# One retention kernel, two changes to its state: full-array products become two quarter-array products, and four small state updates become two

## The chip, the cores and the metric

The kernel runs on one core of a Trainium2 chip. The metric is the device time of one execution in microseconds; a profiled execution also gives the span from its first to its last instruction. The engines are named as in the profile: PE is the matrix engine (PEld its weight loads), DVE the vector engine, ACT the scalar engine, POOL the fourth compute engine, SP the engine that issues all transfers here.

## The reference, cut to what matters

```python
# q, k, v: (4, 8, 768, 64); w_in 512x2048, w_out 2048x512, twice
state = zeros((B, H, D, D))
for t in range(S):
    state = gamma[h] * state + k_t (outer) v_t
    y[:, :, t] = scale * (q_t @ state)
x = y as (B*S, H*D)                     # 3072 tokens x 512
x = leaky_relu(x @ w_in) @ w_out        # first block, factor 0.01
x = elu(x @ w_in2) @ w_out2             # second block
```

Here gamma is 1 - 2^(-5-h) for head h. The weights arrive as 64-bit floats and are converted on the chip.

## The kernel before, in words

**The dense part.** The 3072 tokens are handled in 6 blocks of 512. Each step takes one of 16 slices of 128 hidden features: `gemm1` makes h from the block's x (12 products), `leaky` or the elu functions make g, `split_g` splits it into a high and a low part, and `gemm2`, one to three steps later in `drain`, multiplies by the second weight (12 products). A pair of `gemm1` and `gemm2` is 24 products of 512 columns.

**The retention part.** It runs in chunks of 128 tokens: 24 chunks, 6 of them to a sequence, and for each chunk two units of four heads, so 48 units w = 0 to 47. Unit w has chunk c = w // 2, and i = w % 2 says which two pairs of heads. A unit is written in two halves. `att_a` multiplies queries and keys into scores `sc` (four products, rows 0 to 63 of the array for one head of a pair, rows 64 to 127 for the other) and DVE multiplies them with the mask into `pt`. `att_b` adds up the output `o` in PSUM: q times the state of the chunk before (line 384, only where the chunk is not a sequence's first), then `pt` times v (line 387), and beside it the new k-v product of the chunk (line 391, not for a sequence's last chunk). ACT copies the output to `xhi`, DVE updates the state `st` (line 399, or line 402 where it begins) and then writes `xlo` (line 403). `prep_q` and `prep_k` scale q and k on POOL.

`st` holds for each of the four pairs of heads a 128x128 matrix whose two diagonal 64x64 quarters are the states of the two heads; the other two quarters are zeros, written once on POOL at the start. One product with it serves both heads, and the update has four instructions in a unit, one for each head:

```python
for p, a, r, rs in pairs:               # rs: partitions and columns of head r
    nc.vector.scalar_tensor_tensor(out=st[rs, a, rs], in0=st[rs, a, rs], scalar=gamma[2 * a + r] ** C,
                                   in1=o[rs, p, 1, :D], op0=ALU.mult, op1=ALU.add)
```

**The order.** Every engine works through its instructions in the order of the program. `att_step` runs `att_a` of unit w+1 and `att_b` of unit w, with operations of `conv` between them: `conv` converts the first block's weights, chunk by chunk (16 chunks; lines 95 to 120, on ACT, DVE and POOL). Units 0 to 7 come before any dense step, units 8 to 15 lie two to a step in the first four dense steps, and the other 32 come one to a step or one to two steps from visit 3 on (a visit is a run of steps on one block of tokens). `load_w` and `att_load` issue the transfers of weights (`raw`) and of k, q, v (`kv`) on SP, in program order; the load of `kv` for chunk 6 waits there for chunk 4 to be done, and the fifth `raw` is behind it. `warm` issues products whose result nobody reads, two at the start and one after each of units 0 and 1; they read `st`.

Of the kernel before, what the change touches and what calls it, by code (L numbers as in the profile page):

```python
# [19 lines left out]
F32 = mybir.dt.float32  # L20
# [6 lines left out]
ALU = mybir.AluOpType  # L27
PSUM = bass.MemoryType.PSUM

B, H, S, D = 4, 8, 768, 64  # L30
DM, DFF = 512, 2048
P = 128
C = 128
# [3 lines left out]
NP = H // 2  # L37
BLK = 512
# [4 lines left out]
HM = MF // 2  # L43
# [8 lines left out]
@with_exitstack  # L52
def body(ctx: ExitStack, tc: tile.TileContext, kkv, w1, w2, tabs, out):
    nc = tc.nc
    gamma = [1.0 - 2.0 ** (-5.0 - h) for h in range(H)]

    big = ctx.enter_context(tc.tile_pool(name="big", bufs=1))
    wp = ctx.enter_context(tc.tile_pool(name="wp", bufs=1))
    cv = ctx.enter_context(tc.tile_pool(name="cv", bufs=2))
# [250 lines left out]
    with ExitStack() as actx:  # L310
        ab = actx.enter_context(tc.tile_pool(name="ab", bufs=1))
        ap_ = actx.enter_context(tc.tile_pool(name="ap", bufs=2))
        aps = actx.enter_context(tc.tile_pool(name="aps", bufs=1, space=PSUM))
        kv, pt = {}, {}
        st = ab.tile([P, NP, P], F32, name="st")
        nc.gpsimd.memset(st, 0.0)
        tab = ab.tile([P, H * C + NP * C + H], F32, name="tab")
        ktab = tab[:, :H]
        mask = tab[:, H : H + H * C].rearrange("p (i r t) -> p i r t", i=2, r=2)
        qtab = tab[:, H + H * C :].rearrange("p (a t) -> p a t", a=NP)  # L320

        def att_load(c, first=0, last=4):

# [7 lines left out]
        def prep_k(w):  # L331
            c, i = divmod(w, 2)
            if c < NCH and c % NCB < NCB - 1:
                k = kv[c][:, 2, 4 * i * D : 4 * (i + 1) * D].rearrange("p (h d) -> p h d", h=4)
                nc.gpsimd.tensor_tensor(k, k, ktab[:, 4 * i : 4 * i + 4].unsqueeze(2).to_broadcast([P, 4, D]), ALU.mult)
# [35 lines left out]
        def att_b(w):  # L371

            c, i = divmod(w, 2)
            cb = c % NCB
            t = pt.pop(w)
            if w < 2 * CPB and i:
                o = ps.tile([P, 2, 2, C], F32, tag="y2", name="o")
            else:
                o = aps.tile([P, 2, 2, C], F32, tag="o", name="o")
            pairs = [(p, 2 * i + p, r, slice(r * D, (r + 1) * D)) for p in range(2) for r in range(2)]  # L380
            if cb:
                q = qd.pop(w)
                for p in range(2):
                    nc.tensor.matmul(o[:, p, 0, :], st[:, 2 * i + p, :], q[:, p, :], start=(p == 0), stop=False, skip_group_check=True)  # L384
            for p, a, r, rs in pairs:
                v = kv[c][:, 3, a * C + r * D : a * C + (r + 1) * D]
                nc.tensor.matmul(o[rs, p, 0, :], v, t[:, r, p * C : (p + 1) * C], start=(cb == 0 and p == 0), stop=True, skip_group_check=True)  # L387
            if cb < NCB - 1:
                for p, a, r, rs in pairs:
                    hs = slice(a * C + r * D, a * C + (r + 1) * D)  # L390
                    nc.tensor.matmul(o[rs, p, 1, :D], kv[c][:, 2, hs], kv[c][:, 3, hs], start=False, stop=True, skip_group_check=True)
            b, ts = c // CPB % 2, slice(c % CPB * C, (c % CPB + 1) * C)
            ks = slice(2 * i, 2 * i + 2)
            nc.scalar.copy(xhi[b][:, ks, ts], o[:, :, 0, :])
            yield
            if cb < NCB - 1:
                for p, a, r, rs in pairs:
                    if cb:
                        nc.vector.scalar_tensor_tensor(out=st[rs, a, rs], in0=st[rs, a, rs], scalar=gamma[2 * a + r] ** C,  # L399
                                                       in1=o[rs, p, 1, :D], op0=ALU.mult, op1=ALU.add)  # L400
                    else:
                        nc.vector.tensor_copy(st[rs, a, rs], o[rs, p, 1, :D])
            nc.vector.tensor_tensor(xlo[b][:, ks, ts], o[:, :, 0, :], xhi[b][:, ks, ts].bitcast(F32), ALU.subtract)  # L403
            yield

# [13 lines left out]
        def att_step(before=0, between=0):  # L419


            nonlocal au
            w = au
            c, i = divmod(w, 2)
            scores = att_a(w + 1) if w + 1 < NU else iter((0, 0))
            outputs = att_b(w)
            next(scores)
            conv(before)
            next(scores)
            prep_q(w + 2)  # L430
            next(outputs)
            conv(between)
            next(outputs)
            prep_k(w + 1)
            c_split()
            if i and CPB <= c < NCH - 2:
                att_load(c + 2)
            au += 1

        def warm(n):  # L440

            t = ps.tile([P, BLK], F32, tag="h", name="idle")
            for _ in range(n):
                nc.tensor.matmul(t, st[:, 0, :], st.rearrange("p a e -> p (a e)"), start=True, stop=True)

        au = 0
        warm(2)
        prep_k(0)
        for _ in att_a(0):
            pass  # L450
        for w, (n1, n2) in enumerate(((0, 1), (0, 1), (1, 0), (1, 1), (0, 1), (1, 1), (0, 1), (1, 1))):
            att_step(n1, n2)
            if w < 2:
                warm(1)
# [5 lines left out]
        for s in range(NA):  # L460
            ph, j, m, (_, _, m0, m1, vi) = steps[s]
            n = units.get(vi, 0)
            h = ps.tile([P, BLK], F32, tag="h", name="h")
# [27 lines left out]
    with ExitStack() as ectx:  # L491
# [44 lines left out]
        for s in range(NA, 2 * NS):  # L536
            ph, j, m, (_, _, m0, m1, vi) = steps[s]
            if s % 4 == 0:
                h = ps.tile([P, BLK], F32, tag="h", name="h")
            else:  # L540
                h = eps.tile([P, BLK], F32, tag="h2", name="h2")
# [13 lines left out]
            if (ph, vi) in comes:  # L555
                nx, i = comes[ph, vi], m // 2
# [9 lines left out]
def _tables():  # L566

    gamma = 1.0 - 2.0 ** (-5.0 - np.arange(H, dtype=np.float64))
    t = np.arange(C)
    scale = 1.0 / np.sqrt(D)  # L570
    d = t[None, :] - t[:, None]
    mask = np.where(d >= 0, scale * gamma[:, None, None] ** np.maximum(d, 0), 0.0)
    qtab = scale * gamma[:, None] ** (t + 1.0)
    ktab = gamma[:, None] ** (C - 1.0 - t)
    tab = np.zeros((P, H * C + NP * C + H), np.float32)
    tab[:, :H] = ktab.T

    mask = mask.reshape(2, 2, 2, C, C).transpose(3, 0, 2, 1, 4)
    tab[:, H : H + H * C] = mask.reshape(P, H * C)
    rows = np.repeat(qtab.reshape(NP, 2, 1, C), D, axis=2).reshape(NP, P, C)  # L580
    tab[:, H + H * C :] = rows.transpose(1, 0, 2).reshape(P, NP * C)
    return tab


# [33 lines left out]
```

## Time and profile before

| | |
|---|---|
| time, median of 3 runs | 1206.05 us (1205.2 to 1210.15) |
| the profiled execution's own time | 1206.01 us |
| its span | 1204.2 us |
| mean granted PE clock | 0.989 |
| PE busy | 1172.1 us, 97% of the span |
| DVE, ACT, POOL busy | 682.6, 544.6, 167.8 us |

The busy times are sums over stretches with different limits, so they are to be read stretch by stretch. Products are pipelined, and one product of 32-bit operands (not of the rounded kind that the dense part uses) stands as two records in the trace: the 80 products of line 384 are 160 records.

### The profile page before, as it was taken

What the parts mean: (1) busy time and instruction counts of PE and PEld (TensorE: products, weight loads), DVE (VectorE), ACT (ScalarE), POOL (GpSimd) and SP (SyncE); (2) the same over time, 40 slices, a digit from 0 to 9 for tenths busy, and PEclk for the clock granted to TensorE, in tenths of its full rate; (3) what the DMA queues carried; (4) which work ended last, traced back from release to release, by engine and by line L of the source; (5) the groups of instructions that cost most, each with busy time, mean ns of one, the idle gap of its engine ahead of it and who ended that gap; (6) DMA issues with size and microseconds to landing.
All of it is one profiled execution on the core that took longest, in us unless ns stands there. A gap on an engine that the chain in (4) does not pass through costs nothing.

```text
span 1204.2 us, 14902 instructions
## 1 busy us (share of the span) xinstructions
PE 1172.1 (97%) x5864; PEld 949.1 (79%) x5864; DVE 682.6 (57%) x1169; ACT 544.6 (45%) x913; POOL 167.8 (14%) x145
## 2 busy tenths in 40 slices
PE   6798899999999999999999999999999999999998
PEld 4576778877777777877888888888888888888887
DVE  5988871424564556364211365666665665666665
ACT  2445542222443444343222455555555555564554
POOL 2566520101332133132000000000000000000000
PEclk8799999999999999999999999999999999999999
DMA  9156030333553355352255610000000010000000
GB/s 374 71 222 268 1 99 7 106 105 123 193 192 140 140 193 184 131 188 94 62 182 193 225 54 18 35 18 18 35 18 18 36 35 1 35 1 1 36 1 35
DMA packets 32822, 117.10 MB, mean 97 GB/s; under 512 B 3184, under 2 KB 3184, under 8 KB 25712
## 3 DMA queue, kind: packets, MB, share of 16 engines
q1 hardware_dynamic: 32752, 116.15, 26.7%
q8 instruction: 46, 0.75, 0.3%
q14 instruction: 24, 0.20, 0.0%
HBM read 84.68 MB, written 31.46 MB: 96 GB/s over the span
## 4 chain that ended last, share of the span: by engine, by line
PE 81%; DVE 11%; ACT 4%; DMA 2%; issue 2%; SPq 0%; ACTq 0%; DVEq 0%
PE h L227 37%; PE y L248 37%; PE sc L359 2%; PE o L387 2%; PE o L384 2%; DMA raw<-in_w 2%; DVE f L116 1%; DVE st L399 1%; DVE s L98 1%; DVE f L109 1%; DVE f L105 1%; ACT gf L306 1%; DVE xlo L403 1%; DVE e L113 1%; DVE glo L234 1%
## 5 line engine op out<-in xcount | busy, mean ns | idle before, releaser
L227 PE MATMUL h<-xhi,w 128*128 128x512 f32 x1536 | 513.0, 395 | 10.4 <-ACT gf L306 9.0
L234 DVE TENSOR_TENSOR glo<-gf,ghi 128x512 fp32r<-128x512 f32 x180 | 134.8, 749 | 422.5 <-ACT ghi L233 422.5
L227 PEld LDWEIGHTS h<-xhi,w 128*128 128x128 f32 x1536 | 289.2, 188 | 81.3 <-ACT gf L306 18.7
L227 PE MATMUL h<-xlo,w 128*128 128x512 f32 x768 | 300.9, 392 | 2.5 <-DVE xlo L403 2.4
L248 PE MATMUL y<-ghi,w 128*128 128x512 f32 x768 | 252.4, 389 | 0.1
L248 PE MATMUL y<-w,ghi 128*128 128x512 f32 x768 | 236.4, 389 | 0.0
L227 PEld LDWEIGHTS h<-xlo,w 128*128 128x128 f32 x768 | 144.9, 189 | 32.5 <-DVE xlo L403 4.2
L248 PEld LDWEIGHTS y<-ghi,w 128*128 128x128 f32 x768 | 144.2, 188 | 30.9 <-DVE ysb L281 0.8
L248 PEld LDWEIGHTS y<-w,ghi 128*128 128x128 f32 x768 | 144.1, 188 | 29.9
L514 ACT ACTIVATE n<-h 128x512 f32<-128x512 f32 x96 | 57.4, 598 | 224.4 <-PE h L227 224.4
L248 PE MATMUL y<-glo,w 128*128 128x512 f32 x384 | 149.4, 389 | 0.0
L248 PE MATMUL y<-w,glo 128*128 128x512 f32 x384 | 149.4, 389 | 0.0
L306 ACT ACTIVATE gf<-h 128x512 f32<-128x512 f32 x96 | 57.0, 594 | 163.7 <-PE h L227 163.7
L233 ACT CAST ghi<-gf 128x512 fp32r<-128x512 f32 x192 | 117.6, 613 | 6.0 <-DVE gf L525 3.4
L248 PEld LDWEIGHTS y<-w,glo 128*128 128x128 f32 x384 | 72.1, 188 | 15.1
L248 PEld LDWEIGHTS y<-glo,w 128*128 128x128 f32 x384 | 72.1, 188 | 14.8
L102 ACT ACTIVATE e<-e,ebias 128x512 int16<-128x512 uint16 (+1 forms) x48 | 41.5, 865 | 75.5 <-DVE e L99 75.5
L522 DVE SCALAR_TENSOR_TENSOR a<-n,a 128x512 f32<-128x512 f32 x96 | 65.7, 684 | 5.9 <-ACT n L517 5.9
L524 DVE SCALAR_TENSOR_TENSOR t<-a,t 128x512 f32<-128x512 f32 x96 | 66.4, 692 | 3.3
L525 DVE SCALAR_TENSOR_TENSOR gf<-h,t 128x512 f32<-128x512 f32 x96 | 66.4, 691 | 3.3
L120 POOL TENSOR_TENSOR raw<-f,raw 128x512 fp32r<-128x512 f32 x32 | 41.0, 1281 | 194.3 <-ACT raw L119 185.5
L523 DVE SCALAR_TENSOR_TENSOR t<-n,t 128x512 f32<-128x512 f32 x96 | 65.7, 685 | 0.0
(48 smaller groups left out, 963.2 us busy)
## 6 DMA issues: line engine op xcount, KB each, us to landing
kv<-in_kkv SPq DMA_DIRECT2D x23, 1024.0 KB, 5.3
raw<-in_w SPq DMA_DIRECT2D x16, 1024.0 KB, 9.1
raw<-in_w SPq DMA_DIRECT2D x32, 512.0 KB, 3.6
wscr<-raw SPq DMA_DIRECT2D x32, 512.0 KB, 3.0
w<-wscr SPq DMA_DIRECT2D x16, 1024.0 KB, 4.8
xs<-yscr SPq DMA_DIRECT2D x12, 512.0 KB, 3.8
out<-osb SPq DMA_DIRECT2D x24, 256.0 KB, 2.3
yscr<-ysb SPq DMA_DIRECT2D x16, 256.0 KB, 2.8
```

Source lines behind the costliest of these rows:

```text
L102: nc.scalar.activation(e.bitcast(I16), e, AF.Relu, bias=ebias, scale=2.0**3)
L120: nc.gpsimd.tensor_tensor(lo, f, hi.bitcast(F32), ALU.subtract)
L227: nc.tensor.matmul(h, a, x, start=(n == 0), stop=(n == 3 * KD - 1))
L233: nc.scalar.copy(ghi, gf)
L234: eng.tensor_tensor(glo, gf, ghi.bitcast(F32), ALU.subtract)
L248: nc.tensor.matmul(acc[d], lhsT, rhs, start=(first and n == 0), stop=(last and n == 2))
L306: nc.scalar.activation(gf, h, AF.Prelu, alpha=0.01)
L514: nc.scalar.activation(n, h, AF.Relu, scale=-1.0)
L522: nc.vector.scalar_tensor_tensor(out=a, in0=n, scalar=1.0, in1=a, op0=ALU.add, op1=ALU.mult)
L523: nc.vector.scalar_tensor_tensor(out=t, in0=n, scalar=1.0, in1=t, op0=ALU.add, op1=ALU.mult)
L524: nc.vector.scalar_tensor_tensor(out=t, in0=a, scalar=2.0, in1=t, op0=ALU.add, op1=ALU.mult)
L525: nc.vector.scalar_tensor_tensor(out=gf, in0=h, scalar=0.0, in1=t, op0=ALU.max, op1=ALU.add)
```

## The change

`st` becomes 128 partitions x 4 x 64: the two heads of a pair lie one above the other, and there are no zeros. The product with q takes one 64x64 quarter of the array for each head, four products in a unit where there were two. The update takes both heads of a pair at once, two instructions of 128x64 in a unit where there were four of 64x64; the decay comes from 8 more columns of the table `tab`, as a value for each partition. Where a state begins, one copy of 128x128 takes the place of four of 64x64. The products of `warm` read a tile of zeros, `zeros`, that lies in the buffer of weight chunk 8 until that is loaded.

```diff
-        st = ab.tile([P, NP, P], F32, name="st")
-        nc.gpsimd.memset(st, 0.0)
-        tab = ab.tile([P, H * C + NP * C + H], F32, name="tab")
+        st = ab.tile([P, NP, D], F32, name="st")
+        tab = ab.tile([P, H * C + NP * C + 2 * H], F32, name="tab")
...
+        gtab = tab[:, H + H * C + NP * C :]
...
             if cb:
                 q = qd.pop(w)
-                for p in range(2):
-                    nc.tensor.matmul(o[:, p, 0, :], st[:, 2 * i + p, :], q[:, p, :], start=(p == 0), stop=False, skip_group_check=True)
+                for p, a, r, rs in pairs:
+                    nc.tensor.matmul(o[rs, p, 0, :], st[rs, a, :], q[rs, p, :], start=(p == 0), stop=False, skip_group_check=True)
...
             if cb < NCB - 1:
-                for p, a, r, rs in pairs:
-                    if cb:
-                        nc.vector.scalar_tensor_tensor(out=st[rs, a, rs], in0=st[rs, a, rs], scalar=gamma[2 * a + r] ** C,
-                                                       in1=o[rs, p, 1, :D], op0=ALU.mult, op1=ALU.add)
-                    else:
-                        nc.vector.tensor_copy(st[rs, a, rs], o[rs, p, 1, :D])
+                if cb:
+                    for p in range(2):
+                        a = 2 * i + p
+                        nc.vector.scalar_tensor_tensor(out=st[:, a, :], in0=st[:, a, :], scalar=gtab[:, a : a + 1],
+                                                       in1=o[:, p, 1, :D], op0=ALU.mult, op1=ALU.add)
+                else:
+                    nc.vector.tensor_copy(st[:, ks, :], o[:, :, 1, :D])
...
             t = ps.tile([P, BLK], F32, tag="h", name="idle")
             for _ in range(n):
-                nc.tensor.matmul(t, st[:, 0, :], st.rearrange("p a e -> p (a e)"), start=True, stop=True)
+                nc.tensor.matmul(t, zeros[:, :P], zeros, start=True, stop=True)
 
         au = 0
+        zeros = wp.tile([P, BLK], F32, tag=f"w{HM}", name="zeros")
+        nc.gpsimd.memset(zeros, 0.0)
```

What this does to the instructions shows on PE between units 0 and 2 (the end of unit 0's output, the idle product behind it, the scores of unit 2, the output of unit 1, the next idle product, the scores of unit 3 and the output of unit 2). Before, with what each instruction waits for (DMAHW is a transfer's queue, Pool the engine POOL):

```order
L391 MATMUL o<-kv 64x64 [waits Pool_49]
L391 MATMUL o<-kv 64x64 x3
L444 MATMUL idle<-st 128x512 [waits DVE_49,PE_49]
L359 MATMUL sc<-kv 128x128 [waits DMAHW5_49,PE_49]
L359 MATMUL sc<-kv 128x128 x3
L387 MATMUL o<-pt,kv 64x128 x4
L391 MATMUL o<-kv 64x64 [waits Pool_49]
L391 MATMUL o<-kv 64x64 x3
L444 MATMUL idle<-st 128x512 [waits DVE_49,PE_49]
L359 MATMUL sc<-kv 128x128 x4
L384 MATMUL o<-qd,st 128x128 x2
```

The same place on PE in the changed program:

```order
L389 MATMUL o<-kv 64x64 [waits Pool_49]
L389 MATMUL o<-kv 64x64 x3
L443 MATMUL idle<-zeros 128x512 [waits PE_49]
L357 MATMUL sc<-kv 128x128 [waits DMAHW5_49,PE_49]
L357 MATMUL sc<-kv 128x128 x3
L385 MATMUL o<-pt,kv 64x128 [waits DVE_49] x2
L385 MATMUL o<-pt,kv 64x128 x2
L389 MATMUL o<-kv 64x64 [waits Pool_49]
L389 MATMUL o<-kv 64x64 x3
L443 MATMUL idle<-zeros 128x512 [waits PE_49]
L357 MATMUL sc<-kv 128x128 x4
L382 MATMUL o<-qd,st 64x128 [waits DVE_49]
```

Nothing changes its place. The idle product no longer waits for DVE; the first product that waits for the state is now that of unit 2.

## Rows read from the trace of the kernel before

**Rows 1.** Busy time by stretch: stretch, length, PE, PEld, DVE, ACT, POOL, PE clock, DMA.

```profile
0.00:85.00 85.00, 67.10 (x512) 49.61 (x512) 65.50 (x130) 30.41 (x43) 44.52 (x43) 0.86 0.54 210
85.00:171.00 86.00, 77.95 (x330) 62.05 (x330) 72.32 (x68) 46.87 (x61) 40.00 (x18) 0.98 0.40 150
171.00:608.00 437.00, 434.45 (x2411) 347.02 (x2412) 199.25 (x444) 155.88 (x269) 83.23 (x84) 1.00 0.38 132
```

**Rows 2.** Chain of waits, 200 to 300 us: start, length, what; one unit's pieces.

```profile
209.33 0.65 PE sc L359 x8
209.98 0.64 PE o L384 x4
210.62 0.59 PE o L387 x8
```

**Rows 3.** Chain of waits, shares by line, of 10 to 51 us and 70 to 86 us.

```profile
by line: DMA raw<-in_w 19.6%; DVE st L399 14.0%; PE o L387 7.8%; PE idle L444 7.7%; DVE xlo L403 7.3%; DVE s L98 6.6%; PE sc L359 6.6%; PE o L384 6.0%; DVE f L116 5.5%; DVE pt L367 4.4%; DVE st L402 4.4%; issue 4.3%; PE h L227 3.5%; DVE pt 
...
by line: DVE s L98 15.9%; DVE pt L367 11.8%; DVE st L399 9.9%; DVE f L109 8.7%; PE y L248 8.5%; DVE xlo L403 8.0%; DVE f L105 7.7%; PE h L227 7.5%; DVE f L116 7.1%; DVE st L402 5.0%; PE sc L359 4.2%; DVE e L113 3.7%; issue 3.5%; DVE e L99 0
```

**Rows 4.** Timeline, units 0 to 2: start, length, engine, instruction, idle time before.

```profile
12.10 0.92 DVE L402 COPY st<-o 64x64 f32<-64x64 f32 x4
...
13.17 2.05 PE L444 MATMUL idle<-st 128*128 128x512 f32 x2 [4.27 <-DVE st L402]
13.33 0.73 POOL L344 TENSOR_TENSOR qd<-kv,tab 128x256 f32<-128x256 f32 x1 [4.93 <-DMA kv<-in_kkv]
14.02 0.61 POOL L335 TENSOR_TENSOR kv<-kv,tab 128x256 f32<-128x256 f32 x1
...
15.15 1.23 PE L359 MATMUL sc<-kv 64*128 64x128 f32 x8
...
18.22 0.72 POOL L344 TENSOR_TENSOR qd<-kv,tab 128x256 f32<-128x256 f32 x1 [2.34 <-DMA kv<-in_kkv]
...
19.12 1.10 PE L444 MATMUL idle<-st 128*128 128x512 f32 x2 [1.53 <-DVE st L402]
...
22.77 0.91 DVE L399 SCALAR_TENSOR_TENSOR st<-st,o 64x64 f32<-64x64 f32 x4 [1.12 <-ACT xhi L394]
```

**Rows 5.** Timeline of DVE, 36 to 39 us.

```profile
36.35 0.74 DVE L365 TENSOR_TENSOR pt<-sc,tab 128x256 f32<-128x256 f32 x2
...
37.61 0.91 DVE L399 SCALAR_TENSOR_TENSOR st<-st,o 64x64 f32<-64x64 f32 x4
38.53 0.42 DVE L403 TENSOR_TENSOR xlo<-o,xhi 128x256 fp32r<-128x256 f32 x1
```

**Rows 6.** Groups by line and shape: count, busy us, mean ns, idle before.

```profile
L399 DVE SCALAR_TENSOR_TENSOR st<-st,o 64x64 f32<-64x64 f32 x128 | 27.9, 218 | 22.7 <-ACT xhi L394 21.2
...
L102 ACT ACTIVATE e<-e,ebias 128x1024 int16<-128x1024 uint16 x16 | 18.4, 1149 | 42.2 <-DVE e L99 42.2
L95 ACT COPY e<-raw 128x1024 int16<-128x1024 int16 x16 | 17.9, 1119 | 13.7 <-DMA raw<-in_w 13.7
...
L365 DVE TENSOR_TENSOR pt<-sc,tab 128x256 f32<-128x256 f32 x8 | 3.0, 417 | 0.3 <-PE sc L359 0.3
```

**Rows 7.** Timeline of PE, one unit at full clock.

```profile
303.62 0.66 PE L387 MATMUL o<-pt,kv 128*64 128x128 f32 x8
304.11 0.40 PE L391 MATMUL o<-kv 128*64 128x64 f32 x8
```

**Rows 8.** Chain of waits, 0 to 70 us.

```profile
51.67 6.86 DMA raw<-in_w
...
60.53 1.20 PE o L384 x4
```

**Rows 9.** Timeline, DVE and POOL side by side, two places.

```profile
40.60 0.42 DVE L98 TENSOR_SCALAR s<-e 128x1024 uint16<-128x1024 uint16 x1
...
74.86 2.37 POOL L120 TENSOR_TENSOR w<-f,w 128x1024 fp32r<-128x1024 f32 x1 [2.38 <-ACT w L119]
...
74.89 2.62 DVE L98 TENSOR_SCALAR s<-e 128x1024 uint16<-128x1024 uint16 x1
```

More of the change, by code (lines that the diff above doesn't have):

```diff
@@ L54, in body @@
     nc = tc.nc
-    gamma = [1.0 - 2.0 ** (-5.0 - h) for h in range(H)]
     big = ctx.enter_context(tc.tile_pool(name="big", bufs=1))
@@ L314, in body @@
         kv, pt = {}, {}
-        st = ab.tile([P, NP, P], F32, name="st")
-        nc.gpsimd.memset(st, 0.0)
-        tab = ab.tile([P, H * C + NP * C + H], F32, name="tab")
+        st = ab.tile([P, NP, D], F32, name="st")
+        tab = ab.tile([P, H * C + NP * C + 2 * H], F32, name="tab")
         ktab = tab[:, :H]
         mask = tab[:, H : H + H * C].rearrange("p (i r t) -> p i r t", i=2, r=2)
-        qtab = tab[:, H + H * C :].rearrange("p (a t) -> p a t", a=NP)
+        qtab = tab[:, H + H * C : H + H * C + NP * C].rearrange("p (a t) -> p a t", a=NP)
+        gtab = tab[:, H + H * C + NP * C :]
         def att_load(c, first=0, last=4):
@@ L574, in _tables @@
     ktab = gamma[:, None] ** (C - 1.0 - t)
-    tab = np.zeros((P, H * C + NP * C + H), np.float32)
+    tab = np.zeros((P, H * C + NP * C + 2 * H), np.float32)
     tab[:, :H] = ktab.T
@@ L580, in _tables @@
     rows = np.repeat(qtab.reshape(NP, 2, 1, C), D, axis=2).reshape(NP, P, C)
-    tab[:, H + H * C :] = rows.transpose(1, 0, 2).reshape(P, NP * C)
+    tab[:, H + H * C : H + H * C + NP * C] = rows.transpose(1, 0, 2).reshape(P, NP * C)
+    tab[:, H + H * C + NP * C :][:, :NP] = np.repeat(gamma.reshape(NP, 2) ** C, D, axis=1).T
     return tab
```

## The prediction

> **What bounds the kernel now.** I read the busy time by stretch first [rows 1]. The kernel has two regimes. From 171 us on PE is busy 434.45 of 437 us, at full clock, and to the end little else happens; whatever is taken from PE there comes off the time, and nothing else does. In the first 171 us PE has gaps (67.10 busy of 85, 77.95 of 86) and a clock of 0.86 in the first half, while DVE has 65.50 and 72.32: here a chain through DVE decides. So I asked the chain of waits for both. Between 200 and 300 us a retention unit stands in it with its PE pieces alone: 0.65 us of scores, 0.64 us for q times state, 0.59 us for `pt` times v [rows 2]; DVE's update is not in it. Between 10 and 51 us the chain is mixed: 14.0% of it, 5.7 us, are updates on line 399, 7.7% are idle products, 4.4% the copies on line 402; between 70 and 86 us updates have 9.9% and a copy 5.0% [rows 3]. Behind 86 us the same chain runs through the conversion of weights on DVE and ACT. What is saved before 86 us therefore reaches the end if the conversion starts earlier by as much.
>
> The profiled execution took 1206.01 us, the median is 1206.05, so the sums below need no correction; 1.8 us of it lie outside the span.
>
> **The idle products: the start.** Before, the idle product behind unit 0 read `st`, so it waited for the four copies of that unit (12.10 + 0.92) and stood 4.27 us; the scores of unit 2, queued behind it, began at 15.15 [rows 4]. Now it can begin when unit 0's output is done, at 13.17 - 4.27 = 8.9 us, and with 1.10 to 2.05 us it is over by 11. The scores of unit 2 then wait for their `kv`, which POOL's scaling of q saw landing at 13.33, so they begin 1.85 us earlier. I leave them their 1.23 us (half clock), since PE rests here as before. Unit 1's output then ends at 15.8 instead of 19.12 - 1.53 = 17.6; its k-v product needs POOL's k, ready at 14.02 + 0.61 = 14.63, which holds nothing. The second idle product waited those 1.53 us for unit 1's copies; it now begins at 15.8, takes 1.10, and the scores of unit 3 start at 16.9, where 19.12 + 1.10 = 20.2 stood. All behind it moves by about 3.3 us, the update of unit 2 from 22.77 to 19.5. The next floor is the `kv` of chunk 2, seen at 18.22, and unit 4's scores would come just behind that. **Term: -3.3 us.** Bounds: -1.5 if only the first wait gives something, -4.3 if the clock stays up and the scores need 0.65.
>
> **The updates.** Four 64x64 instructions take 0.91 us, and `xlo` begins 0.92 us after the first [rows 5]: one begins when the one before it ends, 0.23 apart. Two mask products on all partitions, of 0.417 us each [rows 6], take 0.74 together [rows 5]: the second begins some 0.08 us before the first is over. The length of a DVE instruction goes with the columns (0.23 for 64 columns in the copies [rows 4], 0.42 for 256 in `xlo`), not the partitions, so one 128x64 update takes the 0.218 us of a 64x64 one [rows 6]. If the new ones overlap as the mask products do, `xlo` begins 2 x 0.15 = 0.30 us after the first update: 0.62 us saved in a unit, 0.48 if they do not. That the decay now comes from a value for each partition has no row; ACT's nearest pair, with such a bias and without, differs by 1.149 - 1.119 = 0.03 us [rows 6]; I take nothing, at most 0.06 a unit. A copy of 128 columns lies between the 0.23 and the 0.42, at 0.29, or 0.21 to the next: 0.71 us saved of 0.92.
>
> How many count? In 10 to 51 us the 5.7 us are seven updates, in 70 to 86 us it is two and one copy [rows 3]; the copies of units 0 and 1 are in the first term, and the other copy and one update lie where DVE waits for a weight transfer or for PE. That gives 9 x 0.62 + 0.71 = 6.3. Once DVE is that much quicker it will meet ACT's copy of the output (it waited 1.12 us for that at 22.77 [rows 4]), so I take **-6.0 us**; bounds -3 (every second one is given to such a wait) and -6.3. The 6.86 us from issue to landing of the fifth `raw` [rows 8] stay, but its issue follows unit 9 and moves with it. From 171 us on 22 more updates get shorter for nothing, because PE covers them; without this cover each would be worth the same 0.62.
>
> **The quarter products.** In a unit two products of 128x128 (four records) become four of 64x64 (eight records). No row shows a quarter. Rows and columns halved singly are there: the scores use 64 rows by 128 columns and run eight records in the 0.65 us in which line 384 runs four [rows 2], so two row halves run side by side. Line 387 uses 128 rows by 64 columns for the same 128 moving columns, and its eight records take 0.49 us from start to start [rows 7] or 0.59 in the chain: two column halves run side by side too. The two heads' quarters differ in rows and columns both. If they run side by side, a unit costs what line 387 costs, 0.54 us between its two figures: 0.10 saved. Bounds: 0.49 (0.15 saved), 0.64 (nothing), and taking turns, below. From visit 3 on there are 32 units, and 4 of them (chunks 12 and 18) begin a sequence and have no such product: 28 x 0.10 = **-2.8 us**, all of it on PE's path [rows 1]. In the early chain line 384 has 6.0% of 41 us [rows 3] and 1.20 us at 60.53 [rows 8], 3.7 us in all with the slow clock; a sixth of that, less unit 2's part, is **-0.5 us**.
>
> The Trainium skill, TensorEngine Tiling (Array Packing), section Gotcha 1: PSUM Pressure, speaks against this: different row tiles cannot access the same PSUM bank at the same time. Both quarters write one bank here, on different partitions; in the rows above the scores' two row halves write two banks, and line 387's column halves one. No run yet shows the case; by this rule of the Trainium skill it would be the first rival below.
>
> **What else changes.** The memset of `zeros` takes the place of that of `st` on POOL. The tile lies in the buffer of the ninth weight chunk, whose load comes up in the fifth dense step, long after the last idle product. The table's second part grows by 4 KB; two `kv` blocks of 1 MB land 4.9 us apart at this point (13.33 and 18.22 [rows 4]), so that is 0.01 us. Nothing is queued behind a new wait.
>
> **Sum:** 3.3 + 6.0 + 0.5 + 2.8 = 12.6; 1206.0 - 12.6 = **1193.4 us**.
>
> **Rivals.**
> *The quarters take turns.* If the pair does not overlap, eight records cost twice line 387's 0.49, 0.98 us, or as many whole-array records, 8 x 0.16 = 1.28. In the 28 units that adds 9.5 to 17.9 us; the four units of the early chain, two of them at half clock, count like six and add 2 to 3.8. With the first two terms, -9.3, the time is 1208 to 1218, in the middle 1213. It is slower than before from a unit price of 0.64 + 9.3 / 34 = 0.91 us on. For it: both quarters write one bank, and no row has two row halves that do. Against it: both kinds of halves overlap, and different partitions are written.
>
> *The early gain is given back.* The stretch from 85 to 171 us is a chain of DVE, ACT and POOL, and where POOL's `L120` runs, DVE's `L98` took 2.62 us instead of 0.42 [rows 9]. A shifted start can make more such meetings: three more are 6.6 us. Then 1198 to 1203 remain. For it: POOL is busy 40.00 and DVE 72.32 of 86 us there [rows 1], so meetings are many and their number is luck. Against it: order and transfers all move together, so the old pattern should come again.
>
> *The update was not what was waited for.* If POOL or PE sets the early pace, the second term is 3 or less and the first 1.5: 1206.0 - 1.5 - 3 - 0.5 - 2.8 = 1198.2, or 1203.2 with the last term alone.
>
> **How the numbers follow.** The forecast, with its own range 1189 to 1198, gets 0.62. The second and third rival together, 1198 to 1203, get 0.22, the quarters in turns 0.10, a gain beyond 1189 0.04, and 0.02 is left for other losses. From 1189 to 1203 there is 0.84, so that is the range. 0.5% is 6 us, about what a measurement of this kernel can tell from no change: faster means below 1200.0, slower above 1212.1. Half of the 0.22 lies below 1200: faster 0.62 + 0.04 + 0.11 = 0.77; of the turns half are within 6 us: same 0.11 + 0.05 = 0.16; slower 0.05 + 0.02 = 0.07.
>
> **What would show it.** The scores of unit 2 near 13.3 us and unit 2's update near 19.5; two updates in about 0.36 us and `xlo` 0.30 us behind the first; the stretch in which PE is never idle starting near 161 instead of 171 us; between it and 600 us the product with q in 0.49 to 0.59 us a unit in the chain. The forecast is wrong if that product takes 0.9 us or more, or if the full stretch begins later than 166 us.

## The result, and the profile after

The changed kernel takes 1194.84 us (median of 6 runs, 1194.06 to 1196.19) against 1207.57 us for the kernel before in the same series (6 runs, 1205.2 to 1210.43). The ratio is 0.9894, with a 95% interval of 0.9875 to 0.9913: about 12.7 us faster. The profiled execution took 1194.88 us, its span is 1193.1 us.

The kernel before spreads over some 6 us from run to run (1205.3 to 1211.5 in the largest series, of 29 runs); its profiled execution, 1206.01 us, lies near the lower end. So a difference between two traces can be off by some of that spread. Where it can arise shows in the trace of the quarter products alone (below), which up to unit 2 is the same program on PE and took 1210.0 us. There the second idle product, 1.10 us in [rows 4], stands as

```profile
19.37 2.05 PE L444 MATMUL idle<-st 128*128 128x512 f32 x2 [1.53 <-DVE st L402]
```

The granted clock from 19.0 to 21.3 us was 0.50 (1.2 GHz) there and 1.00 (2.4 GHz) in the kernel before, after nearly the same work: PE busy from 13.2 us on, then waiting 1.53 us. Unit 2's update began at 25.55 us instead of 22.77; the trace is 3.9 us behind at the first of the two marks used below, and 4.0 at the end. That the runs of the kernel before differ among themselves for the same reason is likely, not shown.

The busy time of the changed kernel by stretch, in the columns of [rows 1]:

```profile
0.00:85.00 85.00, 69.36 (x580) 51.33 (x581) 63.00 (x104) 33.47 (x47) 43.49 (x44) 0.90 0.58 230
85.00:161.00 76.00, 69.71 (x295) 55.89 (x294) 62.30 (x57) 41.81 (x55) 37.18 (x18) 0.98 0.38 141
161.00:597.00 436.00, 433.81 (x2539) 347.56 (x2538) 190.65 (x392) 157.90 (x272) 85.29 (x85) 1.00 0.38 133
```

The third line looks as in [rows 1]: PE busy nearly throughout. It will turn out that this line hides most of what the result has to teach. Two transfers on SP mark the stretch off better, since every version issues them at the same place in the program: the first reload of a partial sum, when the early part is over, and the first store of the last block of the first phase. From the timeline of SP, the kernel before:

```profile
167.92 0.80 SPq L289 DMA_DIRECT2D ysb<-pscr  x2
...
595.55 2.20 SPq L282 DMA_DIRECT2D yscr<-osb  x4
```

and the changed kernel:

```profile
163.00 10.92 SPq L287 DMA_DIRECT2D ysb<-pscr  x4
...
584.41 2.20 SPq L280 DMA_DIRECT2D yscr<-osb  x4
```

The first mark came 4.9 us earlier and the second 11.1 us earlier. So the stretch between them, called the middle stretch from here on, shrank from 427.63 to 421.41 us, by 6.2 us, where 2.8 were forecast; and the early part gave 4.9 us in these two traces, where 9.8 were forecast. The sum came out near the forecast, the place did not.

The start, from the timeline of the changed kernel, against [rows 4]:

```profile
8.81 1.12 PE L443 MATMUL idle<-zeros 128*128 128x512 f32 x2
...
13.61 0.73 POOL L342 TENSOR_TENSOR qd<-kv,tab 128x256 f32<-128x256 f32 x1 [5.23 <-DMA kv<-in_kkv]
13.62 1.22 PE L357 MATMUL sc<-kv 64*128 64x128 f32 x8 [3.67 <-DMA kv<-in_kkv]
...
16.24 1.52 PE L443 MATMUL idle<-zeros 128*128 128x512 f32 x2
...
20.26 0.47 DVE L398 SCALAR_TENSOR_TENSOR st<-st,tab,o 128x64 f32<-128x64 f32 x2 [1.07 <-ACT xhi L392]
```

The idle product no longer waits, the scores of unit 2 wait for their `kv` instead (13.62 in place of 15.15), and unit 2's update starts 2.5 us earlier. The new groups by line and shape (count, busy us, mean ns, idle before), against [rows 6]:

```profile
L382 PE MATMUL o<-qd,st 64*64 64x128 f32 x320 | 27.6, 293 | 1.9 <-DVE xlo L402 1.8
...
L398 DVE SCALAR_TENSOR_TENSOR st<-st,tab,o 128x64 f32<-128x64 f32 x64 | 15.0, 275 | 18.5 <-ACT xhi L392 18.4
...
L401 DVE COPY st<-o 128x128 f32<-128x128 f32 x8 | 2.3, 285 | 2.0 <-ACT xhi L392 2.0
```

An update takes 275 ns where a 64x64 one took 218. The timeline of DVE shows what a unit pays, against [rows 5]:

```profile
23.32 0.47 DVE L398 SCALAR_TENSOR_TENSOR st<-st,tab,o 128x64 f32<-128x64 f32 x2
23.70 0.41 DVE L402 TENSOR_TENSOR xlo<-o,xhi 128x256 fp32r<-128x256 f32 x1
```

`xlo` begins 0.38 us behind the first update, where it was 0.92: 0.54 us saved in a unit.

One unit in the chain of waits of the changed kernel, 200 to 235 us, against [rows 2]:

```profile
204.41 0.65 PE sc L357 x8
205.06 0.58 PE o L382 x8
205.64 0.59 PE o L385 x8
206.23 0.23 PE o L389 x8
206.46 2.99 PE h L225 x12
...
212.17 0.65 PE sc L357 x8
```

and, from the chain of the kernel before, the two pieces behind those of [rows 2] that close its period:

```profile
211.44 2.95 PE h L227 x12
...
217.11 0.65 PE sc L359 x8
```

The product with q takes 0.58 us instead of 0.64, but the h behind the unit takes 2.99 instead of 2.95. From scores to scores it is 7.76 us instead of 7.78.

The gain of the middle stretch lies elsewhere. The chain of the kernel before between 302 and 324 us, a part whose chain the prediction had not looked at:

```profile
303.05 0.64 PE o L384 x4
...
304.56 0.38 ACT xhi L394
...
305.65 0.22 DVE st L399
305.89 0.42 DVE xlo L403
...
308.28 0.70 DVE f L116
...
309.13 0.62 ACT raw L119
309.76 0.50 ACT gf L306
...
310.30 3.04 PE h L227 x12
...
323.96 3.01 PE h L227 x12
```

Here PE is not what the chain runs on. From the unit's output it goes to ACT's copy, to DVE's four updates and `xlo`, through DVE's conversion of the second block's weights to line 116, from there to ACT's rounding copy of these weights (line 119), and only behind that copy, in ACT's order, comes `leaky` (line 306), which frees the buffer that the next h needs. PE waits for it at 310.30. The period of two steps and a unit is 13.66 us. The same part of the changed kernel:

```profile
298.52 2.99 PE h L225 x12
301.50 2.72 PE y L246 x12
304.22 2.72 PE h L225 x12
306.94 2.72 PE y L246 x12
309.66 0.65 PE sc L357 x8
...
311.71 2.99 PE h L225 x12
```

Now the chain is PE alone, and the period is 13.19 us. Counted over the whole stretch, the waits of h's weight loads for `leaky` (us in total, times, longest us) are before, from 171 to 608 us,

```profile
PEld h L227 <- ACT gf L306: 10.2, 15, 1.9
```

and in the changed kernel, from 160 to 597 us,

```profile
PEld h L225 <- ACT gf L304: 4.3, 5, 1.9
```

Ten of the 15 waits are gone, and 5.9 us of waiting with them, where the stretch lost 6.2.

### The profile page after: what moved, and what is told of

It reads as the page before. It is cut to its first block, busy times and chain, and to the rows that moved or that the text cites. A ratio compares the mean times of both kernels' runs of the same rounds, so it can differ in the third digit from the quotient of the medians.

```text
span 1193.1 us, 15132 instructions
## 1 busy us (share of the span) xinstructions
PE 1165.4 (98%) x6024; PEld 945.0 (79%) x6024; DVE 661.4 (55%) x1081; ACT 544.6 (46%) x913; POOL 166.0 (14%) x145
## 4 chain that ended last, share of the span: by engine, by line
PE 87%; DVE 7%; ACT 2%; DMA 2%; issue 1%; SPq 0%; ACTq 0%; DVEq 0%
PE h L225 41%; PE y L246 40%; PE sc L357 2%; PE o L385 2%; PE o L382 2%; DMA raw<-in_w 1%; DVE s L96 1%; DVE f L114 1%; DVE f L107 1%; DMA kv<-in_kkv 1%; DVE glo L232 1%; DVE e L111 1%; PE o L389 1%; DVE e L97 1%; ACT w L117 0%
```

## The experiments

Medians stand against the kernel before run in the same series. The differences between versions use the medians as they are; the kernel before has 1207.5 to 1208.5 us in the five series, so a difference across series can be off by about 1 us for that alone.

**Idle products alone (e1_idle).** The kernel before with these lines:

```diff
-                nc.tensor.matmul(t, st[:, 0, :], st.rearrange("p a e -> p (a e)"), start=True, stop=True)
+                nc.tensor.matmul(t, zeros[:, :P], zeros, start=True, stop=True)
...
+        zeros = wp.tile([P, BLK], F32, tag=f"w{HM}", name="zeros")
+        nc.gpsimd.memset(zeros, 0.0)
```

> The kernel before with the idle products reading zeros, nothing else. If what unit 2's update gained at the start (2.5 us: 22.77 to 20.26) reaches the end, 1204 to 1205 us, about 2.5 below before, and the stretch in which PE is full begins near 168.5 us instead of 171. If the early chain gives it back (the floor is the landing of kv, then POOL and DVE), no change, within 1 us.

Measured: 1204.73 us against 1208.39, ratio 0.9968 (0.9956 to 0.9979). The start's gain reaches the end: 3.7 us by the medians. The trace shows only 1.7 against the trace before: the scores of unit 2 begin 1.75 us earlier, but the second idle product runs at half clock here (0.50 granted from 15.0 to 17.5 us) and takes 2.08 us, and unit 2's update begins at 21.08 instead of 22.77. Against the trace with 2.05 us for that product (25.55) the gain is 4.5 us; the median lies between. The middle stretch is as before, 427.53 us (166.25 to 593.78).

**Quarter products alone (e2_quarter).** The kernel before, on the diagonal blocks of its state tile:

```diff
-                for p in range(2):
-                    nc.tensor.matmul(o[:, p, 0, :], st[:, 2 * i + p, :], q[:, p, :], start=(p == 0), stop=False, skip_group_check=True)
+                for p, a, r, rs in pairs:
+                    nc.tensor.matmul(o[rs, p, 0, :], st[rs, a, rs], q[rs, p, :], start=(p == 0), stop=False, skip_group_check=True)
```

> The kernel before with four quarter products on the diagonal blocks of the same state tile; updates and idle products as before. By the chain of the changed kernel (0.58 instead of 0.64 us a unit) 28 units give 1.7 us, and the early slow-clock ones up to 0.5 more: 2 us below before. By the forecast (0.10 a unit) 3.3 us. If the quarters needed the smaller state tile or the shorter update to overlap, 9 us or more above before.

Measured: 1208.31 us against 1208.39, ratio 1.0001 (0.9988 to 1.0014). None of the three came: the quarter products give nothing that can be measured. They take 0.58 us in the chain here too, and the middle stretch is 427.66 us.

**Four updates everywhere (e3_four_updates), early (e4_four_early), late (e5_four_late).** The changed kernel with the old updates where the condition holds: always, `w < 16`, or `w >= 16`.

```diff
+                if w < 16:
+                    for p, a, r, rs in pairs:
+                        if cb:
+                            nc.vector.scalar_tensor_tensor(out=st[rs, a, :], in0=st[rs, a, :], scalar=gamma[2 * a + r] ** C,
+                                                           in1=o[rs, p, 1, :D], op0=ALU.mult, op1=ALU.add)
+                        else:
+                            nc.vector.tensor_copy(st[rs, a, :], o[rs, p, 1, :D])
-                if cb:
+                elif cb:
                     for p in range(2):
```

> The changed kernel with four updates (and four copies) for each unit, on the small state tile. Theory from the two traces: between 290 and 600 us the update lies on a chain through DVE's conversion and ACT to the next h, so the shorter update is worth about 4.6 us there and 2 to 3 us early: 6.5 to 7.5 us above the changed kernel. Rival, as forecast: worth 6 us early and nothing later: about 6 above too, so this run gives the sum and the next one where it lies.

> The changed kernel with four updates only in units 0 to 15 (the first 85 us), two in all later ones. Theory (the update's gain lies mostly between 290 and 600 us): 2 to 3 us above the changed kernel. Rival, as forecast (PE covers the later updates): all of it, 6 us above.

> The changed kernel with four updates only in units 16 to 47 (from visit 3 on), two in the first 85 us. By the forecast PE covers these updates, and the time stays at 1195. If they lie on the chain from xhi through DVE's conversion and ACT to leaky, the 4.9 us that lie between the runs with four updates everywhere and with four updates early alone come back: 1199.5 to 1200, and the stretch from 163 to 584 us takes some 6 us longer, as in the kernel before.

Measured: 1205.79 us with four updates everywhere (ratio to before 0.9978, 0.9967 to 0.9989), 1200.88 with four early (0.994, 0.9923 to 0.9958), 1201.42 with four late (0.9939, 0.9924 to 0.9953), against 1194.84 with two everywhere. The updates are worth 10 to 11 us (1205.79 - 1194.84 = 11.0, or 10.1 by the two ratios to before), more than either theory had. The late ones are worth 1205.79 - 1200.88 = 4.9 us, or, taken last, 1201.42 - 1194.84 = 6.6; the early ones 1205.79 - 1201.42 = 4.4 or 1200.88 - 1194.84 = 6.0. So my reading after the result, that the early ones give only 2 to 3, was wrong too, and the forecast's 6.0 is at the upper end; the first mark in the four traces says 4.5 (167.49 with four early, 163.00 with two everywhere) or 3.5 (167.78 with four everywhere, 164.28 with four late). The parts do not add up exactly: the start and the quarters together, which is what four updates everywhere leave, give 2.6 us against before, and 2.6 + 11.0 is more than the 12.7 of the whole. The timeline of SP with four updates late shows where theirs go:

```profile
164.28 10.96 SPq L288 DMA_DIRECT2D ysb<-pscr  x4
...
591.88 2.20 SPq L281 DMA_DIRECT2D yscr<-osb  x4
```

The middle stretch is 427.60 us, the length that it has in the kernel before, although quarters and idle products are the new ones, and `leaky` is waited for 15 times again, 10.8 us. With four updates early alone the stretch is 422.80, with 4 such waits, 5.2 us.

**The wait of leaky taken away (e8_defer_before), with the quarters (e11_defer_quarter), and in the changed kernel (e9_defer_after).** The last piece of each conversion is held back and issued behind the next step's `leaky`:

```diff
-        r = t.bitcast(F32R)
-        halves(r[:, :BLK], r[:, BLK:], f)
-        nc.sync.dma_start(out=wscr[m][:, :, a, :], in_=r.rearrange("p (a c) -> p a c", a=2).bitcast(F32))
+        held.append((t.bitcast(F32R), f, m, a))
+
+    held = []
+
+    def pre_end():
+        if held:
+            r, f, m, a = held.pop(0)
+            halves(r[:, :BLK], r[:, BLK:], f)
+            nc.sync.dma_start(out=wscr[m][:, :, a, :], in_=r.rearrange("p (a c) -> p a c", a=2).bitcast(F32))
...
             gf = leaky(h)
+            pre_end()
```

> The kernel before, with one change that is not part of the change under study: the last piece of the second block's weight conversion (ACT's rounding copy on line 119, POOL's rest, the store) is issued one step later, behind that step's leaky. ACT then no longer waits for DVE's conversion ahead of leaky. If the late updates count because of that wait, PE's pauses in front of h between 290 and 600 us go, and the time falls by 4 to 6 us against before. If the pauses have another cause, no change.

> The same deferred piece together with the quarter products, updates and idle products as before. If the quarters' gain (0.06 us a unit) was lost in the pauses, it shows now: 1.5 to 2 us below the run with the deferred piece alone. If the quarters give nothing by themselves, the same time as that run.

> The changed kernel with the deferred piece of the second block's weight conversion. The shorter updates have already taken most of the wait for DVE out of leaky's way: the stretch from 163 to 584 us can lose the 0.3 us by which the deferred kernels were shorter, so 1194.5, no difference that can be measured. If DVE still held PE up there, 2 us or more.

Measured: the kernel before with the deferred piece 1202.84 us against 1208.54, ratio 0.9952 (0.9936 to 0.9967). Its SP timeline:

```profile
168.01 0.80 SPq L295 DMA_DIRECT2D ysb<-pscr  x2
...
589.32 2.20 SPq L288 DMA_DIRECT2D yscr<-osb  x4
```

With four updates in every unit and full products the middle stretch is now 421.31 us, as long as in the changed kernel, and of the 15 waits for `leaky` one is left, which every version has:

```profile
PEld h L233 <- ACT gf L312: 1.9, 1, 1.9
```

What the late updates gave was this wait of `leaky` behind the conversion, as far as these traces can tell: versions with the same late part (two updates, piece not deferred) have middle stretches of 420.03 to 422.80 us, so a cause worth a microsecond beside it would not show. With the quarters on top: 1202.95 us, 0.9955 (0.9942 to 0.9967), middle stretch 421.00; the 1.5 to 2 us that I expected of them do not show even where nothing else hides them. The changed kernel with the deferred piece: 1193.08 us against 1207.46, ratio 0.9877 (0.9857 to 0.9897), middle stretch 419.52 with one wait for `leaky` instead of five. It has the lowest median of the study, 1.8 us below the changed kernel, between the 0.3 and the 2 of the expectation; the two intervals overlap, and the changed kernel with added idle products (below) has 420.03 without any deferring, so whether it is faster than the changed kernel is open.

**The order of the quarters (e7_turns), and one quarter alone (e12_one_quarter).** The changed kernel with

```diff
-                for p, a, r, rs in pairs:
+                for p, a, r, rs in sorted(pairs, key=lambda x: (x[2], x[0])):
```

and, in the other, with

```diff
-                    nc.tensor.matmul(o[rs, p, 0, :], st[rs, a, :], q[rs, p, :], start=(p == 0), stop=False, skip_group_check=True)
+                    nc.tensor.matmul(o[:D, p, 0, :], st[:D, a, :], q[:D, p, :], start=(p == 0 and r == 0), stop=False, skip_group_check=True)
```

In the second, the start flag of the products behind it, on line 385, is set to match.

> The changed kernel with the four quarter products in another order: both of the upper heads, then both of the lower ones, so that neighbours in the program use the same quarter. If two quarters run side by side only when neighbours use different ones, the unit's product goes from 0.58 us towards 0.98 and the time rises by up to 28 x 0.4 = 11 us, to 1206. If PE sorts that out by itself, or the quarters never overlapped, the product stays at 0.58 and the time at 1195.

> The changed kernel with all four state products of a unit on the upper left quarter: the upper head's product is made twice and the lower head's is left out. If the four took 0.58 us because two quarters run side by side, they take more here, up to 0.98 us a unit in the chain between 200 and 300 us. If a quarter product just costs 0.15 us by itself, the 0.58 us stay.

Measured: 1196.2 us for the other order (ratio 0.9899, 0.9883 to 0.9914), the product at 0.59 us in the chain: the order does not matter. With one quarter, 1210.16 us (one run), and in its chain of waits:

```profile
209.83 1.01 PE o L382 x8
...
211.66 2.94 PE h L225 x12
```

So 0.58 us come from two quarters side by side, and on one quarter the same records cost 1.01. In the other order two products on one quarter stand ahead of those on the other, and still nothing is lost. Were their records begun in that order, four on the first quarter would begin before any on the second; at 1.01 / 8 = 0.13 us a record the second quarter could begin 0.38 us in and would need 0.5 more, some 0.88 us by this estimate, where 0.59 was measured. So the records of the second pair do overtake; whether PE does this, or a step between the program and PE, no run here tells.

**The decay as a constant (e6_immediate).**

```diff
-scalar=gtab[:, a : a + 1],
+scalar=(1.0 - 2.0 ** (-5.0 - 2 * a)) ** C,
```

> The changed kernel with the decay as a constant in the instruction instead of a value for each partition; the constant is that of the pair's first head, so the second head's state decays wrongly. If the value for each partition is what makes an update 275 ns instead of 218, the updates fall to 218 ns, and nine on the early path give 1 us: 1194. If the length comes from the 128 partitions, 275 ns and no change.

Measured: 1195.82 us, ratio 0.9898 (0.9881 to 0.9915); the updates' mean is 214 ns. The value for each partition does cost 0.06 us an instruction, and the time does not show it: the 1 us that was expected is within the spread, and the median is 1.0 above the changed kernel's, not below.

**The clock in the early part (e10_warm).**

```diff
-            if w < 2:
+            if w < 2 or w in (5, 6):
                 warm(1)
```

> The changed kernel with one more idle product of zeros behind each of units 5 and 6. PE's clock is at half in part of 28 to 36 us and of 43 to 48 us, where one output (0.58 + 0.59 + 0.26 us at full clock) took 1.12 + 1.05 + 0.45. If the idle products keep the clock up there, up to 1.2 us less; if their 1 us each stands ahead of scores that DVE waits for, up to 1 us more.

Measured: 1195.29 us, ratio 0.9892 (0.9873 to 0.9911): no difference. The busy time of 28 to 36 us, in the columns of [rows 1], first with the added idle products,

```profile
28.00:36.00 8.00, 7.62 (x80) 5.14 (x81) 8.00 (x17) 3.09 (x5) 5.54 (x7) 1.00 0.21 86
```

and in the changed kernel:

```profile
28.00:36.00 8.00, 7.21 (x77) 5.84 (x78) 8.00 (x17) 3.18 (x5) 5.79 (x7) 0.79 0.22 90
```

The clock is full where it was 0.79, but DVE was busy 8.00 of 8 us before and is still: there the clock was not what was waited for. In the other place, 43.5 to 48 us, the clock stayed at 0.62 with the added product, so that half of the question is not answered.

## Why the prediction was right, and where it was not

The time, 1194.8 us for a forecast of 1193.4, and the sign are right. It puts a price on four things: the start, the early updates, the late ones and the quarters. The first two held in size, and the other two failed in opposite directions, so that the sum came as near as it did partly by luck: 4.9 to 6.6 us that were put at nothing stand where 2.8 + 0.5 were put that did not come.

**The start: right by the medians.** Forecast 3.3 us, measured 3.7 with the idle products alone (2.5 to 5.3 by the interval). In the changed kernel's trace unit 2's scores started at 13.62, with their `kv`, for a forecast of 13.3. Its update was at 20.26, not 19.5: 0.3 us of that are the scores' start, and most of the rest is PE's half clock, which reached further, so that the second idle product took 1.52 us, not 1.10. The prediction had a clock that stays up among its bounds (-4.3), but none that stays down longer; with the clock at either level the traces give 1.7 to 4.5 us for the same edit.

**The early updates: near in size, not in count.** Forecast 6.0 us, measured 4.4 to 6.0 by the medians and 3.5 to 4.5 by the traces. A unit saves 0.54 us, between the two bounds of 0.48 and 0.62. The overlap came as read from the mask products (two that take 0.275 each are over in 0.47, and `xlo` begins 0.38 behind the first), but the value for each partition, which I had put at nothing and at most 0.06 a unit, costs 0.06 for each of the two instructions. What the forecast had too high is how many units pass the saving on. From unit 2's update to unit 9's it is 29.67 us before (22.77 to 52.44) and 27.45 in the changed kernel (20.26 to 47.71): 2.2 us saved in seven steps, where 0.62 each would be 4.3. Three of the seven steps save 0.54 us or more, one 0.24, the others next to nothing.

In the two traces the early part together, start, updates and quarters, gave only 4.9 us, little more than half of what the start and the early updates have by the medians. Part of this is which trace of the kernel before one takes, since the profiled one is near the lower end; how much is not shown. The text of the prediction called itself wrong if the full stretch began later than 166 us. The chain's piece of h that began it at 170.96 before begins in the changed kernel at

```profile
166.04 3.01 PE h L225 x12
```

so by that mark it is just wrong, and with reason: the early part gave less in the trace than was forecast, and what followed had to come from somewhere else.

**The late updates: the step that failed.** "From 171 us on 22 more updates get shorter for nothing, because PE covers them." They gave 4.9 to 6.6 us, as much as the early ones (with no cover at all 22 x 0.62 = 13.6 us were to come). The step rested on [rows 1], where PE is busy 434.45 of 437 us, and on a chain taken from 200 to 300 us [rows 2]. Both mislead in the same way. The second block's weights are converted only from 291 to 559 us, and it is this conversion that stands between DVE's update and `leaky`; a chain taken from 300 to 400 us would have shown it, as the rows above do. And PE's busy time is made of records that overlap: neighbours begin 0.23 us apart and last 0.39. The last product of y before the h at 310.30 begins at 309.79, 0.51 us ahead of it, so PE lost 0.28 us, but only 0.12 of that count as idle. The weight loads' waits for `leaky`, 15 of them, would have shown it. Deferring ACT's copy took the same 6.3 us off the middle stretch with the updates left alone (427.63 to 421.31), and with four late updates the stretch is back at 427.60. That settles the cause.

**The quarters: over-sized.** Forecast 2.8 us late and 0.5 early, measured nothing (0.1 us below before, with an interval of some 1.5 us to either side; with the piece deferred, 0.1 above). The mechanism is as forecast: two quarters run side by side, 0.58 us against 1.01 on one quarter. The size was wrong twice. The unit's product costs 0.58, not 0.54; and 0.04 of the 0.06 us that this saves are lost again in the next h, 2.99 against 2.95 us. The remaining 0.02 us times 28 is 0.6 us at most, below what can be measured here. Why the h behind it is longer I did not find out; with one quarter alone it is 2.94.

**The rivals.** The quarters taking turns did not happen; one quarter alone, at 1210.16 us (one run), shows what it would have cost, and lies in that rival's 1208 to 1218. The rule of the Trainium skill that spoke for it (TensorEngine Tiling (Array Packing), section Gotcha 1: PSUM Pressure: different row tiles cannot access one PSUM bank at the same time) does not hold these products apart: both write one bank, on different partitions, and they overlap. The early gain was not given back from 85 us on: unit 15's update starts 4.3 us earlier in the changed kernel (79.17 for 83.50) and the first mark comes 4.9 earlier. That the early update was not what was waited for is refuted as a whole by the runs with four updates early and late, 4.4 to 6.0 us; for about half of the steps from unit 2 to unit 9 it holds.

## What to carry to other kernels

Take the chain of waits separately in every part of the program in which a different side job runs, not once for a stretch in which one engine looks full: here one chain from 200 to 300 us stood for 300 us more, in which a conversion had begun and the answer was another. An engine that is 99% busy by its records may still pause in every other step; look at the start of the first product behind each hand-over, and at what stands ahead of the releasing instruction in its own engine's order. Saving on a small product pays only what is left from one unit's scores to the next's, not the difference of its own piece.

## What the runs showed of the hardware

- Two 64x64 quarters on the diagonal run side by side although they write one PSUM bank on different partitions: 0.58 us for eight records, 1.01 on one quarter, and 0.59 with the products in an order in which neighbours share a quarter. The next group of twelve dense products took 2.99 us behind two quarters and 2.94 behind one.
- An update on DVE with a value for each partition takes 275 ns where the same with a constant takes 214.
- Two DVE updates on all partitions overlap in their records, 0.47 us from the first start to the last end for 2 x 0.275, while four that alternate between the partition halves took 0.91 for 4 x 0.218 [rows 5, 6].
- PE's granted clock from 19.0 to 21.3 us was 1.00 in one trace and 0.50 in another behind nearly the same work: the same idle product took 1.10 us and 2.05, and unit 2's update began 2.8 us later in the second.
